# A decode step on one core: w1 in one transfer, w2's first products queued behind V, small constants made on GpSimd

## The chip, the cores and the metric

The kernel runs on one core of one Trainium2 chip. The time is that of the device for one execution, in microseconds (us). A quoted time is the median of several executions on the same chip; the four of each kernel in the first session agree within 0.3% (132.57 to 132.89 us before, 132.71 to 132.92 us changed). A ratio is the mean time of one kernel's runs over the mean time of the other kernel's runs of the same rounds, so it is not quite the ratio of the medians beside it. Executions over 1.5% slower than the fastest of the same kernel are left out of the means.

The core has TensorE (PE; PEld is its weight load), VectorE (DVE), ScalarE (ACT), GpSimd (POOL) and SyncE (SP, which issues most DMA transfers), and 16 DMA engines. A transfer is issued when SyncE gives the order for it. In the trace of the kernel before it gives the orders one after the other, and that for w2's first half (61.08 us) only after a wait of 4.5 us for VectorE's transposes of the block whose space it fills; the order for V's next to it comes at 61.46 us. A transfer then waits in the queue behind those issued earlier: the first packet of w2's first half starts at 64.08 us, while the last packet of K ends at 65.73 us. The engines move it in packets, and each packet has its start, length and size in the trace. The granted clock is the share of TensorE's full clock that the trace shows.

## The reference, cut to what matters

```python
# x: 1x576.  W = 4096 last positions of the cache, 32 query heads, 16 kv heads, Dh = 128
q = x @ wq                                  # wq 576 x 4096
p = softmax(q . k[:, Sk-W:] / sqrt(128))    # 16 x 4096 x 128 of K are read
a = (p . v[:, Sk-W:]) @ wo                  # the same of V; wo 4096 x 576
b = gelu(x @ w1 + b1) @ w2 + b2             # w1 576 x 4608, w2 4608 x 576
g = sigmoid(sum(x * gate_w))
out = g * a + (1 - g) * b
```

One token is computed, so every weight and every cache row is used once. All inputs are bf16; 53.6 MB must come from memory.

## The kernel before

```python
# small rows, issued from ScalarE's queue: x, gate_w, b2, b1
nc.scalar.dma_start(out=x_row, ...)         # ... three more
# large loads, issued from SyncE in this order: w1, wq, K (8 x 2 MB), w2 first half, V (4 x 4 MB), wo, w2 second half
for i0, i1 in ((0, 4), (4, NI)):
    nc.sync.dma_start(out=w1_t[:, i0:i1, :], in_=w1_src[:, i0:i1, :])
nc.sync.dma_start(out=wq_t[:, ...], ...)
# ... constants (identity, parity masks, permutation) on VectorE from one identity matrix ...
# TensorE: h = b1 + x w1 (162 products), q = x wq (144), then scores
for g in range(NG):
    k_t = big.tile([P, 2, SL, Dh], BF16, name="k_t", tag="CDBA"[g])
    # per half: load, two VectorE transposes (2.3 us each), 16 products into s_ps
# ... softmax: maximum on VectorE, two small products, exp on ScalarE, transposes ...
w2_t = big.tile([P, NF, D], BF16, name="w2_t", tag="B")      # the third K block's space
nc.sync.dma_start(out=w2_t[:, 0:NJ, :], in_=w2_src[:, 0])
for g in range(NG):
    v_t = big.tile([P, NCK, Dh], BF16, name="v_t", tag="CDAC"[g])
    # load 4 MB, 128 products into o_ps
# ... wo, and w2's second half in pieces of 10, 6 and 2 rows ...
for f in range(6):
    y_add(gt[:, f : f + 1], w2_t[:, f, :])      # two products of 288 columns each
# ... ov = om . lo32b ...
for f in range(6, NJ):
    y_add(gt[:, f : f + 1], w2_t[:, f, :])
for r in range(RO):
    y_add(ov[:, r : r + 1], wo_t[:, r, :])
for f in range(NJ, NF):
    y_add(gt[:, f : f + 1], w2_t[:, f, :], stop=(f == NF - 1))
```

The scheduler places the 36 products of w2's first half (f below 18) where their data are ready, not where the text has them. In the kernel before that is during the softmax.

## Time and profile before

132.79 us, median of 3 runs (132.57 to 132.89).

| what | value | where it is read |
|---|---|---|
| bytes moved, mean rate | 53.76 MB, 410 GB/s | page |
| K stage, 32 to 64 us | 425 GB/s at a DMA share of 1.00 | table of stretches |
| busy: TensorE, VectorE, ScalarE, GpSimd | 60, 42, 10, 1% of the span | page |
| last weights usable | 128.27 us | chain of waits |

Three rows of the page, the span of 131.2 us in 40 equal slices: granted TensorE clock and DMA share in tenths (9 is 90% or more), and the rate.

```profile
PEclk9999999999999999999999998555555555555589
DMA  7999999899999999999999999989989999999980
GB/s 242 407 454 407 472 466 427 381 425 415 430 425 420 430 440 412 420 440 420 423 462 469 410 390 480 450 380 450 475 380 415 480 385 418 404 422 420 410 330 15
```

The transfers fill the span; nothing else does. The end of the chain of waits (start, length, what) says the same of the finish: a transfer, 16 products, a cast.

```profile
103.54 24.73 DMA w_t<-in_B_w_dram
...
128.31 1.19 PE y_ps L268 x16
129.50 0.43 DVE out_row L515
```

Lines of the timeline (start, length, engine, line, operation, count, idle time before it and what ended that):

```profile
12.85 10.21 PE L294 MATMUL h_ps<-x,w_t 128*128 128x2 bf16 x162
...
26.91 4.00 PE L332 MATMUL q_ps<-x,wq_t 128*128 128x2 bf16 x144 [3.86 <-DMA wq_t<-in_A_wq_dram]
...
61.08 0.33 SPq L443 DMA_DIRECT2D w_t<-in_B_w_dram  x1
...
72.74 1.14 PE L268 MATMUL y_ps<-w_t,gt 128*1 128x288 bf16 x15
...
76.76 0.35 PE L414 MATMUL mb_ps<-ones,mh 1*128 1x1 f32 x2
...
77.34 1.39 ACT L427 ACTIVATE p_t<-s_ps,negm 128x512 bf16<-128x512 f32 x1 [44.78 <-DVE negm L418]
...
117.23 4.00 PE L268 MATMUL y_ps<-wo_t,ov 128*1 128x288 bf16 x32 [1.32 <-DMA wo_t<-in_A_wo_dram]
122.74 3.44 PE L268 MATMUL y_ps<-wo_t,ov 128*1 128x288 bf16 x32 [1.51 <-DMA wo_t<-in_A_wo_dram]
...
128.31 1.15 PE L268 MATMUL y_ps<-w_t,gt 128*1 128x288 bf16 x16 [0.71 <-DMA w_t<-in_B_w_dram]
```

The products of w2's first half start at 72.7 us. Behind V, TensorE waits for wo twice and for w2 once. The wo products go at about 125 ns each (32 in 4.00 us), where the granted clock is 0.5.

### The profile page before, as it was taken

How to read it: one execution, taken by the hardware profiler on the slowest of the kernel's cores; microseconds unless marked ns; L12 is line 12 of the kernel's file. 1: busy time of each engine (PE TensorE's matmuls, PEld its weight loads, DVE VectorE, ACT ScalarE, POOL GpSimd, SP SyncE). 2: the span in 40 equal slices, each digit the busy share in tenths (PEclk: the TensorE clock that was granted, in tenths of full speed). 3: DMA queues.
4: the chain of work that ended last, by engine and by line, in shares of the span. 5: the costliest groups of instructions: out<-in, count | busy, mean ns of one | idle time of the engine just before them, and what ended most of it. 6: DMA issues, size and time to landing. Idle time of an engine off the chain costs nothing.

```text
span 131.2 us, 2379 instructions
## 1 busy us (share of the span) xinstructions
PE 79.0 (60%) x1126; PEld 45.2 (34%) x1062; DVE 55.4 (42%) x80; ACT 13.0 (10%) x25; POOL 0.7 (1%) x6
## 2 busy tenths in 40 slices
PE   0037999075599969769769560006573910949583
PEld 0034999074012212112112140006573910934351
DVE  6059100503988988988986720745000000010001
ACT  3000000003000000000000049950000000000001
POOL 2000000000000000000000000000000000000000
PEclk9999999999999999999999998555555555555589
DMA  7999999899999999999999999989989999999980
GB/s 242 407 454 407 472 466 427 381 425 415 430 425 420 430 440 412 420 440 420 423 462 469 410 390 480 450 380 450 475 380 415 480 385 418 404 422 420 410 330 15
DMA packets 3045, 53.76 MB, mean 410 GB/s; under 512 B 342, under 2 KB 346, under 8 KB 604
## 3 DMA queue, kind: packets, MB, share of 16 engines
q1 hardware_dynamic: 3026, 53.61, 96.4%
q8 instruction: 8, 0.13, 0.4%
q10 hardware_dynamic: 10, 0.01, 0.0%
q14 instruction: 1, 0.01, 0.0%
HBM read 53.62 MB, written 0.00 MB: 409 GB/s over the span
## 4 chain that ended last, share of the span: by engine, by line
DMA 65%; PE 13%; DVE 8%; ACT 8%; issue 4%; SPq 1%; DVEq 0%
DMA k_t<-in_A_k_cache_dram 26%; DMA wq_t<-in_A_wq_dram 20%; DMA w_t<-in_B_w_dram 19%; ACT p_t L427 7%; PE o_ps L476 5%; DVE kt L375 3%; PE q_ps L332 3%; DVE pt L435 2%; DVE m L397 2%; PE s_ps L385 1%; PE y_ps L268 1%; SPq L489 1%; PE t_ps L451 0%; DVE out_row L515 0%; SPq L491 0%
## 5 line engine op out<-in xcount | busy, mean ns | idle before, releaser
L375 DVE STREAM_TRANSPOSE kt<-k_t 128x2048 f32<-128x2048 f32 x16 | 36.0, 2290 | 9.4 <-DMA k_t<-in_A_k_cache_dram 9.4
L385 PE MATMUL s_ps<-kt,qz_flat 128*128 128x512 bf16 x128 | 32.8, 404 | 8.6 <-DVE kt L375 8.6
L476 PE MATMUL o_ps<-pt,v_t 128*128 128x8 bf16 x512 | 14.4, 168 | 10.7 <-issue 7.6
L385 PEld LDWEIGHTS <-qz_flat 128*128 128x128 bf16 x64 | 6.5, 102 | 34.2 <-issue 33.0
L476 PEld LDWEIGHTS <-v_t 128*128 128x128 bf16 x512 | 14.3, 104 | 10.9 <-issue 7.8
L427 ACT ACTIVATE p_t<-s_ps,negm 128x512 bf16<-128x512 f32 x8 | 9.7, 1415 | 44.8 <-DVE negm L418 44.8
L494 DVE TENSOR_TENSOR om<-o_ps,rgh 128x128 bf16<-128x128 f32 x1 | 0.3, 292 | 24.2 <-PE o_ps L476 24.2
L294 PE MATMUL h_ps<-x,w_t 128*128 128x2 bf16 x162 | 10.2, 202 | 0.0
L294 PEld LDWEIGHTS <-w_t 128*128 128x128 bf16 x162 | 10.1, 163 | 0.0
L268 PE MATMUL y_ps<-wo_t,ov 128*1 128x288 bf16 x64 | 7.4, 420 | 2.8 <-DMA wo_t<-in_A_wo_dram 2.8
L451 PE MATMUL t_ps<-ls,ones 128*128 128x32 f32 x2 | 0.6, 396 | 11.9 <-DVE ls L449 11.9
L435 DVE STREAM_TRANSPOSE pt<-p_t 128x2048 bf16<-128x2048 bf16 x2 | 4.6, 2312 | 7.4 <-ACT p_t L427 7.4
L332 PE MATMUL q_ps<-x,wq_t 128*128 128x2 bf16 x144 | 4.0, 166 | 3.9 <-DMA wq_t<-in_A_wq_dram 3.9
L515 DVE CAST out_row<-y_ps 1x288 bf16<-1x288 f32 x1 | 0.4, 446 | 13.4 <-PE y_ps L268 13.4
L268 PEld LDWEIGHTS <-ov 128*1 128x1 bf16 x64 | 3.9, 118 | 6.1 <-issue 2.8
L268 PE MATMUL y_ps<-w_t,gt 128*1 128x288 bf16 x72 | 5.6, 285 | 0.7 <-DMA w_t<-in_B_w_dram 0.7
L332 PEld LDWEIGHTS <-wq_t 128*128 128x128 bf16 x144 | 3.9, 104 | 3.9 <-DMA wq_t<-in_A_wq_dram 3.9
L195 PE MATMUL xs_ps<-one_b,rows 1*128 1x1 bf16 x9 | 0.7, 195 | 7.3 <-DVE rows L192 7.3
L451 PEld LDWEIGHTS t_ps<-ls,ones 128*128 128x128 f32 x2 | 0.5, 310 | 12.2 <-issue 12.2
L514 ACT CAST out_row<-y_ps 1x288 bf16<-1x288 f32 x1 | 0.4, 391 | 42.5 <-PE y_ps L268 42.5
L303 DVE COPY hacc<-h_ps 128x36 f32<-128x36 f32 x1 | 0.2, 195 | 9.4 <-PE h_ps L294 9.4
L268 PEld LDWEIGHTS <-gt 128*1 128x1 bf16 x72 | 3.2, 82 | 2.8 <-issue 1.8
(68 smaller groups left out, 28.7 us busy)
## 6 DMA issues: line engine op xcount, KB each, us to landing
k_t<-in_A_k_cache_dram SPq DMA_DIRECT2D x8, 2048.0 KB, 30.4
v_t<-in_A_v_cache_dram SPq DMA_DIRECT2D x4, 4096.0 KB
wq_t<-in_A_wq_dram SPq DMA_DIRECT2D x1, 4608.0 KB, 25.7
wo_t<-in_A_wo_dram SPq DMA_DIRECT2D x2, 2304.0 KB, 20.1
w_t<-in_B_w_dram SPq DMA_DIRECT2D x1, 2880.0 KB, 14.1
w_t<-in_B_w_dram SPq DMA_DIRECT2D x1, 2592.0 KB, 11.3
w_t<-in_B_w_dram SPq DMA_DIRECT2D x1, 2304.0 KB
w_t<-in_B_w_dram SPq DMA_DIRECT2D x1, 1440.0 KB, 23.1
```

Source lines behind the costliest of these rows:

```text
L195: nc.tensor.matmul(xs_ps[:, i : i + 1], lhsT=xdup[:, i : 2 * D : NI], rhs=one_b[0:1, 0:1], start=(i == 0), stop=(i == NI - 1), skip_group_ ...
L268: nc.tensor.matmul(y_out[s], lhsT=vec, rhs=row[:, s * DH : (s + 1) * DH], start=start, stop=stop, skip_group_check=True,)
L294: nc.tensor.matmul(h_ps[:, j:NF:NJ], lhsT=w1_t[:, i, j:FH:NJ], rhs=x2[:, i, :], start=False, stop=(i == NI - 1 and j == NJ - 1), skip_grou ...
L332: nc.tensor.matmul(q_ps[:, j : Hq : Hq // 2], lhsT=wq_t[:, i, j * Dh : (j + 1) * Dh], rhs=x2[:, i, :], start=(i == 0 and j == 0), stop=(i ...
L375: nc.vector.transpose(out=kt[:, u * half : (u + 1) * half].bitcast(FP32), in_=k_t[:, f, u * SL // 2 : (u + 1) * SL // 2, :] .rearrange("p ...
L385: nc.tensor.matmul(s_ps[:, u * 512 : (u + 1) * 512].rearrange("p (c k) -> p c k", k=32), lhsT=qz[:, h0 // 2, j, :], rhs=kv[:, u * SL // 4 ...
L397: nc.vector.reduce_max(out=m2[:], in_=s_ps[:].rearrange("p (n b) -> p b n", b=2), axis=AX.X)
L427: nc.scalar.activation(out=p_t[:, cs, :, b], in_=s_ps[:].rearrange("p (c k u b) -> p u b c k", k=8, u=2, b=2)[:, f, b % 2], func=ACT.Exp, ...
L435: nc.vector.transpose(out=pt[:, cs, :].rearrange("p c h -> p (c h)"), in_=p_t[:, cs, :, :].rearrange("p c k b -> p (c k b)"),)
L451: nc.tensor.matmul(t_ps[:], lhsT=ones[:], rhs=ls[:], start=True, stop=True)
L476: nc.tensor.matmul(o_ps[:, 8 * g : 8 * g + 8, 0], lhsT=v_t[:, c, :], rhs=pt[:, c, 8 * g : 8 * g + 8], start=(c == 0), stop=(c == NCK - 1),)
L489: nc.sync.dma_start(out=wo_t[:, r0:r1, :], in_=wo_src[:, r0:r1, :])
```

## The change

The intent: fewer and longer packets for w1 (one row of 41,472 B per partition instead of 18,432 and 23,040 B); the constants taken off VectorE; and the 36 products of w2's first half put behind V in TensorE's queue, so that TensorE does not pause before wo arrives. "V uncut" only removes a loop of one pass.

```diff
-    for i0, i1 in ((0, 4), (4, NI)):
-        nc.sync.dma_start(out=w1_t[:, i0:i1, :], in_=w1_src[:, i0:i1, :])
+    nc.sync.dma_start(out=w1_t[:], in_=w1_src)
 ...
-    nc.vector.memset(ones[:], 1.0)                 # and par, alt, lo32, hi4, lo8, pen, perm on VectorE
+    nc.gpsimd.iota(low[:, c0 : c0 + n], pattern=pattern, base=base, channel_multiplier=1)
+    nc.gpsimd.memset(mask[:, c0 : c0 + n], keep)
+    nc.vector.tensor_tensor(out=low[:], in0=low[:], in1=mask[:], op=ALU.bitwise_and)
+    nc.gpsimd.tensor_scalar(out=is0[:], in0=low[:], scalar1=0.0, scalar2=None, op0=ALU.is_equal)
 ... (perm by affine_select, casts and the two small copies merged, gt in one VectorE instruction)
-    nc.vector.memset(qz_flat[:].bitcast(FP32), 0.0)
+    nc.gpsimd.memset(qz_flat[:].bitcast(FP32), 0.0)
 ...
-    for f in range(6):
-        y_add(gt[:, f : f + 1], w2_t[:, f, :])
+    with tc.issue_after(v_last.ins):
+        for f in range(6):
+            y_add(gt[:, f : f + 1], w2_t[:, f, :])
 ...
-    for f in range(6, NJ):
-        y_add(gt[:, f : f + 1], w2_t[:, f, :])
+    with tc.issue_after(ov_mm.ins):
+        for f in range(6, NJ):
+            y_add(gt[:, f : f + 1], w2_t[:, f, :])
```

More of the change, by code (lines that the diff above doesn't have):

```diff
@@ L11 @@
 BF16 = mybir.dt.bfloat16
+I32 = mybir.dt.int32
 ACT = mybir.ActivationFunctionType
@@ L174 @@
     one_b = const.tile([1, 2], BF16, name="one_b")
-    nc.vector.memset(one_b[:], 1.0)
+    nc.gpsimd.memset(one_b[:], 1.0)
+    NCC = 2 * NI + 32 + 4 + 6
+    low = const.tile([P, NCC], I32, name="low")
+    mask = const.tile([P, NCC], I32, name="mask")
+    c0 = 0
+    for base, pattern, keep in (
+        (0, [[1, NI], [1, 2]], 1),
+        (128, [[-1, 32]], 31),
+        (128, [[-32, 4]], 96),
+        (8, [[-2, HB]], 6),
+        (4, [[-2, 2]], 2),
+    ):
+        n = 1
+        for step, num in pattern:
+            n *= num
+        nc.gpsimd.iota(low[:, c0 : c0 + n], pattern=pattern, base=base, channel_multiplier=1)
+        nc.gpsimd.memset(mask[:, c0 : c0 + n], keep)
+        c0 += n
@@ L176 @@
+    nc.vector.tensor_tensor(out=low[:], in0=low[:], in1=mask[:], op=ALU.bitwise_and)
+    is0 = const.tile([P, NCC], FP32, name="is0")
+    nc.gpsimd.tensor_scalar(
+        out=is0[:], in0=low[:], scalar1=0.0, scalar2=None, op0=ALU.is_equal
+    )
+    alt = is0[:, 0 : 2 * NI].rearrange("p (i t) -> p i t", t=2)
+    lo32 = is0[:, 2 * NI : 2 * NI + 32]
+    hi4 = is0[:, 2 * NI + 32 : 2 * NI + 36]
     ones = const.tile([P, P], FP32, name="ones")
-    nc.vector.memset(ones[:], 1.0)
+    nc.gpsimd.memset(ones[:], 1.0)
@@ L178 @@
     ident = const.tile([P, P], BF16, name="ident")
     make_identity(nc, ident[:])
-    ident_f = const.tile([P, P], FP32, name="ident_f")
-    nc.vector.tensor_copy(out=ident_f[:], in_=ident[:])
-    par = const.tile([P, 2], FP32, name="par")
-    nc.vector.reduce_sum(out=par[:], in_=ident_f[:].rearrange("p (a t) -> p t a", t=2), axis=AX.X)
-    alt = const.tile([P, NI + 1], FP32, name="alt")
-    for t in range(2):
-        nc.vector.tensor_copy(
-            out=alt[:, t : NI + 1 : 2], in_=par[:, t : t + 1].to_broadcast([P, (NI + 1) // 2])
-        )
@@ L191 @@
-    for t in range(2):
-        nc.vector.tensor_copy(out=xdup.rearrange("p (d t) -> p d t", t=2)[:, :, t], in_=x_row)
-    xs_ps = ps_m.tile([P, NI], FP32, name="xs_ps", tag="m")
+    perm = const.tile([P, 4, 4, 32], BF16, name="perm")
+    nc.gpsimd.memset(perm[:], 0.0)
+    nc.gpsimd.affine_select(
+        out=perm[:],
+        in_=perm[:],
+        pattern=[[-64, 2], [-1, 2], [0, 4], [-2, 32]],
+        compare_op=ALU.not_equal,
+        fill=1.0,
+        base=0,
+        channel_multiplier=1,
+    )
@@ new lines @@
+    ident_f = const.tile([P, P], FP32, name="ident_f")
+    nc.gpsimd.tensor_copy(out=ident_f[:], in_=ident[:])
+    lo32b = const.tile([P, 32], BF16, name="lo32b")
+    nc.gpsimd.tensor_copy(out=lo32b[:], in_=lo32)
+    pens = const.tile([P, HB + 2], FP32, name="pens")
+    nc.gpsimd.tensor_scalar(
+        out=pens[:],
+        in0=is0[:, 2 * NI + 36 : NCC],
+        scalar1=1e30,
+        scalar2=-1e30,
+        op0=ALU.mult,
+        op1=ALU.add,
+    )
+    pen = pens[:, 0:HB]
+    pen2 = pens[:, HB : HB + 2]
@@ L194 @@
+    nc.vector.tensor_copy(
+        out=xdup.rearrange("p (d t) -> p d t", t=2),
+        in_=x_row.rearrange("p (d o) -> p d o", o=1).to_broadcast([1, D, 2]),
+    )
+    xs_ps = ps_m.tile([P, NI, 1], FP32, name="xs_ps", tag="m")
     for i in range(NI):
         nc.tensor.matmul(
-            xs_ps[:, i : i + 1],
+            xs_ps[:, i, :],
             lhsT=xdup[:, i : 2 * D : NI],
@@ L203 @@
     x2 = const.tile([P, NI, 2], BF16, name="x2")
-    for t in range(2):
-        nc.vector.tensor_tensor(
-            out=x2[:, :, t], in0=xs_ps[:], in1=alt[:, t : t + NI], op=ALU.mult
-        )
-    lo32 = const.tile([P, 32], FP32, name="lo32")
-    nc.vector.reduce_sum(out=lo32[:], in_=ident_f[:].rearrange("p (a t) -> p t a", t=32), axis=AX.X)
-    lo32b = const.tile([P, 32], BF16, name="lo32b")
-    nc.vector.tensor_copy(out=lo32b[:], in_=lo32[:])
-    hi4 = const.tile([P, 4], FP32, name="hi4")
-    nc.vector.reduce_sum(out=hi4[:], in_=ident_f[:].rearrange("p (a t) -> p a t", t=32), axis=AX.X)
-    lo8 = const.tile([P, 8], FP32, name="lo8")
-    nc.vector.reduce_sum(out=lo8[:], in_=ident_f[:].rearrange("p (a c) -> p c a", c=8), axis=AX.X)
-    pen = const.tile([P, HB], FP32, name="pen")
-    nc.vector.reduce_sum(out=pen[:], in_=lo8[:].rearrange("p (b t) -> p b t", t=2), axis=AX.X)
-    nc.vector.tensor_scalar(
-        out=pen[:], in0=pen[:], scalar1=1e30, scalar2=-1e30, op0=ALU.mult, op1=ALU.add
-    )
-    pen2 = const.tile([P, 2], FP32, name="pen2")
-    nc.vector.reduce_max(out=pen2[:], in_=pen[:].rearrange("p (a b) -> p b a", b=2), axis=AX.X)
-    perm = const.tile([P, 4, 4, 32], BF16, name="perm")
-    idv = ident[:].rearrange("p (b l t) -> p b l t", b=2, t=2)
-    for j in range(4):
-        for b in range(4):
-            nc.vector.tensor_copy(out=perm[:, j, b, :], in_=idv[:, j // 2, :, j % 2])
+    nc.vector.tensor_tensor(
+        out=x2[:], in0=xs_ps[:].to_broadcast([P, NI, 2]), in1=alt, op=ALU.mult
+    )
     s0 = const.tile([1, 1], FP32, name="s0")
@@ L258 @@
     nc.vector.tensor_scalar(
-        out=gh[:, 0, :], in0=hi4[:], scalar1=g_t[:, 0:1], scalar2=None, op0=ALU.mult
+        out=gh[:, 0, :], in0=hi4, scalar1=g_t[:, 0:1], scalar2=None, op0=ALU.mult
     )
@@ L322 @@
     nc.vector.reciprocal(out=r_t[:], in_=e_h[:])
-    p1 = const.tile([P, NF], FP32, name="p1")
-    nc.vector.tensor_tensor(out=p1[:], in0=hacc[:], in1=r_t[:], op=ALU.mult)
     gt = const.tile([P, NF], BF16, name="gt")
-    nc.vector.tensor_scalar(out=gt[:], in0=p1[:], scalar1=omg[:, 0:1], scalar2=None, op0=ALU.mult)
+    nc.vector.scalar_tensor_tensor(
+        out=gt[:], in0=hacc[:], scalar=omg[:, 0:1], in1=r_t[:], op0=ALU.mult, op1=ALU.mult
+    )
     q_ps = ps_m.tile([P, Hq], FP32, name="q_ps", tag="m")
@@ L397 @@
     nc.vector.reduce_max(out=m2[:], in_=s_ps[:].rearrange("p (n b) -> p b n", b=2), axis=AX.X)
-    nc.vector.tensor_tensor(out=m2[:], in0=m2[:], in1=pen2[:], op=ALU.add)
+    nc.vector.tensor_tensor(out=m2[:], in0=m2[:], in1=pen2, op=ALU.add)
     m1 = const.tile([P, 1], FP32, name="m1")
@@ L418 @@
     nc.vector.tensor_tensor(
-        out=negm[:], in0=pen[:], in1=mb_ps[:].to_broadcast([P, HB]), op=ALU.add
+        out=negm[:], in0=pen, in1=mb_ps[:].to_broadcast([P, HB]), op=ALU.add
     )
@@ L448 @@
     ls = const.tile([P, Hq], FP32, name="ls")
-    nc.vector.tensor_scalar(out=ls[:], in0=lo32[:], scalar1=sm[:, 0:1], scalar2=None, op0=ALU.mult)
+    nc.vector.tensor_scalar(out=ls[:], in0=lo32, scalar1=sm[:, 0:1], scalar2=None, op0=ALU.mult)
     t_ps = ps_m.tile([P, Hq], FP32, name="t_ps", tag="m")
@@ L468 @@
         )
-        for u in range(1):
-            n = NCK
-            nc.sync.dma_start(
-                out=v_t[:, u * n : (u + 1) * n, :].rearrange("p c d -> p (c d)"),
-                in_=src[:, :, u * n * Dh : (u + 1) * n * Dh],
-            )
+        nc.sync.dma_start(out=v_t[:].rearrange("p c d -> p (c d)"), in_=src)
         for c in range(NCK):
-            nc.tensor.matmul(
+            v_last = nc.tensor.matmul(
                 o_ps[:, 8 * g : 8 * g + 8, 0],
@@ L496 @@
     )
-    for f in range(6):
-        y_add(gt[:, f : f + 1], w2_t[:, f, :])
+    with tc.issue_after(v_last.ins):
+        for f in range(6):
+            y_add(gt[:, f : f + 1], w2_t[:, f, :])
     ov_ps = ps_m.tile([P, RO], FP32, name="ov_ps", tag="m")
-    nc.tensor.matmul(
+    ov_mm = nc.tensor.matmul(
         ov_ps[:], lhsT=om[:].rearrange("p h a -> p (h a)"), rhs=lo32b[:], start=True, stop=True
```

## The prediction

> **What bounds the kernel now.** The DMA queue. The page counts 53.76 MB at a mean of 410 GB/s, a DMA share of 8 or 9 tenths in nearly every slice, and 65% of the chain that ended last is DMA. In the table of stretches the K stage (32 to 64 us) moves 423 to 428 GB/s at a DMA share of 1.00. The last weight transfer lands at 128.27 us; after it only 16 products (1.15 us), a cast (0.45 us) and the store remain. TensorE is busy 60%, VectorE 42%, and they wait for data.
>
> The queue never runs dry: the third K block is issued at 23.1 us, when transfers up to about 43 us are queued; the last V block at 96.3 us, when queued work reaches about 102 us; wo at 102.2 us, when V lands at 111.7 us.
>
> **What the change does.**
> 1. w1 in one transfer: the same bytes, but 128 packets of 41,472 B instead of 256 of 18,432 and 23,040 B. In the packet records 16,384 B take 614 ns and 32,768 B take 1216 ns, so a packet costs about 12 ns plus its bytes at 27.2 GB/s. Eight packets fewer on each engine save about 0.1 us (an estimate from those records), on the critical path.
> 2. The price: w1's first products wait for all of w1, about 15 us instead of 12.85. They run at 63 ns each (162 in 10.2 us), so they end near 25 instead of 23.06 us, before wq lands at 26.9. Nothing is lost.
> 3. Constants to GpSimd: some 20 small VectorE instructions before 13.7 us go. VectorE then idles 9.4 us before the GELU anyway. GpSimd gets longer and may finish near 10 us; x2 needs its mask by 15 us. Off the path.
> 4. The 36 products of w2's first half now run at 72.7 to 77.9 us, inside the softmax's chain. They leave it, so exp starts up to 0.9 us earlier, which DMA hides. They go behind V: 12 after 115.3 us, 24 after the small ov product. At the granted clock of 0.5 there a product takes about 120 ns (32 in 4.0 us), so 36 need up to 4.3 us; the tail's idle times are 1.3 + 1.5 + 0.7 = 3.5 us (waits for wo and w2). [...] the trace agrees for the tail (uninterrupted from 122.7, granted 1.0 from about 125.8 us). Uninterrupted products from 115.3 us should raise it by about 120 us, so the wo products take some 65 ns rather than 115, and the queue is caught up before 126 us. The last 16 still wait for the last DMA.
> 5. V uncut: the same four transfers as before; no effect.
>
> **Predicted.** 132.79 - 0.1 (packets), and 0 to +0.5 from the tail: 132.7 us, range 132.2 to 133.4. Faster by over 2%: 0.02; same: 0.95; slower: 0.03.
>
> **What would show each step.** Last w2 landing at 128.1 to 128.3 us. h_ps products from about 15 to 25 us. Exp starting before 77. After V, 36 products without idle, clock 1.0 from about 120 us instead of 126, wo products near 65 ns, and TensorE again waiting for DMA before the last 16.
>
> **What would make it wrong.** The clock staying at 0.5 in the tail, or an instruction stall among the queued products (V shows 2.3 us stalls after about 128 products): the end slips 1 to 2 us. Small rows landing so late behind 41 KB packets that wq's products are over 10 us late. The engines finishing the last transfers less evenly.

## The result, and the profile after

132.84 us (132.71 to 132.92, 4 runs) against 132.77 us (132.57 to 132.89, 4 runs); ratio 1.0006, 95% interval 0.9989 to 1.0023. That is the same time. A second session gave 1.0004 (0.9975 to 1.0033).

The page's rows of the changed kernel (span 131.0 us), then its chain of waits, cut:

```profile
PEclk9999999999999999999999965555555555556999
DMA  7999899899999999999999999999999989999980
GB/s 215 481 470 456 362 439 450 356 435 425 420 430 425 425 425 430 430 425 425 440 424 492 400 420 470 410 410 460 425 400 455 460 375 400 433 427 419 407 329 26
```

```profile
1.91 13.59 DMA rows<-in_B_b_dram
...
15.54 1.27 PE h_ps L304 x18
16.82 1.05 PE y_ps L290 x4
17.86 10.14 PE h_ps L316 x162
...
101.27 26.86 DMA w_t<-in_B_w_dram
...
128.17 1.20 PE y_ps L290 x16
129.36 0.43 DVE out_row L534
```

The timeline:

```profile
17.80 10.21 PE L316 MATMUL h_ps<-x,w_t 128*128 128x2 bf16 x162
27.86 3.98 PE L354 MATMUL q_ps<-x,wq_t 128*128 128x2 bf16 x144
...
61.24 0.34 SPq L465 DMA_DIRECT2D w_t<-in_B_w_dram  x1
...
76.98 0.55 PE L436 MATMUL mb_ps<-ones,mh 1*128 1x1 f32 x2 [0.71 <-DVE mh L428]
...
77.76 1.39 ACT L449 ACTIVATE p_t<-s_ps,negm 128x512 bf16<-128x512 f32 x1 [44.22 <-DVE negm L440]
...
119.53 2.63 PE L290 MATMUL y_ps<-wo_t,ov 128*1 128x288 bf16 x32
122.61 2.12 PE L290 MATMUL y_ps<-wo_t,ov 128*1 128x288 bf16 x32 [0.45 <-DMA wo_t<-in_A_wo_dram]
126.07 1.39 PE L290 MATMUL y_ps<-w_t,gt 128*1 128x288 bf16 x20 [1.34 <-DMA w_t<-in_B_w_dram]
128.17 1.15 PE L290 MATMUL y_ps<-w_t,gt 128*1 128x288 bf16 x16 [0.70 <-DMA w_t<-in_B_w_dram]
```

The two ends are the same end: the last 16 products still wait 0.7 us for a transfer, which is usable at 128.13 instead of 128.27 us. In the tail TensorE starts wo 2.3 us later, has caught up by 124.7 us, and waits again. At the front the w1 products begin 5 us later, at 17.8 us, and their first release is not w1 but the small row b1. VectorE is busy 51.8 instead of 55.4 us, GpSimd 5.6 instead of 0.7 us, and neither shows in the time.

### The profile page after: what moved, and what is told of

Same layout as the page of the kernel before. It is cut to its first block, busy times and chain, and to the rows that moved or that the text cites. A ratio compares the mean times of both kernels' runs of the same rounds, so it can differ in the third digit from the quotient of the medians.

```text
span 131.0 us, 2371 instructions
## 1 busy us (share of the span) xinstructions
PE 77.3 (59%) x1126; PEld 44.7 (34%) x1062; DVE 51.8 (40%) x48; ACT 13.0 (10%) x25; POOL 5.6 (4%) x25
## 4 chain that ended last, share of the span: by engine, by line
DMA 57%; PE 22%; DVE 8%; ACT 8%; issue 3%; SPq 1%; ACTq 1%; DVEq 0%
DMA k_t<-in_A_k_cache_dram 26%; DMA w_t<-in_B_w_dram 20%; DMA rows<-in_B_b_dram 10%; PE h_ps L316 8%; ACT p_t L449 7%; PE o_ps L493 5%; DVE kt L397 3%; PE q_ps L354 3%; DVE pt L457 2%; DVE m L419 2%; PE y_ps L290 2%; PE s_ps L407 1%; PE h_ps L304 1%; SPq L506 1%; PE t_ps L473 0%
## 5 line engine op out<-in xcount | busy, mean ns | idle before, releaser
L407 PE MATMUL s_ps<-kt,qz_flat 128*128 128x512 bf16 x128 | 32.0, 397 | 8.6 <-DVE kt L397 8.6
L290 PE MATMUL y_ps<-w_t,gt 128*1 128x288 bf16 x72 | 7.2, 362 | 2.0 <-DMA w_t<-in_B_w_dram 2.0
L290 PE MATMUL y_ps<-wo_t,ov 128*1 128x288 bf16 x64 | 4.8, 306 | 0.4 <-DMA wo_t<-in_A_wo_dram 0.4
L290 PEld LDWEIGHTS <-ov 128*1 128x1 bf16 x64 | 3.1, 91 | 2.2 <-issue 0.7
## 6 DMA issues: line engine op xcount, KB each, us to landing
w_t<-in_B_w_dram SPq DMA_DIRECT2D x1, 2592.0 KB, 11.3
```

Source lines behind the costliest of these rows:

```text
L290: nc.tensor.matmul(y_out[s], lhsT=vec, rhs=row[:, s * DH : (s + 1) * DH], start=start, stop=stop, skip_group_check=True,)
L407: nc.tensor.matmul(s_ps[:, u * 512 : (u + 1) * 512].rearrange("p (c k) -> p c k", k=32), lhsT=qz[:, h0 // 2, j, :], rhs=kv[:, u * SL // 4 ...
```

## The experiments

The theory: the DMA queue bounds the kernel, and all that the change moves lies in time that the queue hides. The rival: parts of the change gain and lose by half a microsecond or more and cancel. A second rival for the front: the chain through b1, w1, wq and K, which the changed kernel's chain of waits lists, is itself a limit.

| run | median us (runs) | before, same rounds | ratio (95%) |
|---|---|---|---|
| w1 whole alone | 132.76 (6) | 132.81 | 0.9999 (0.9962 to 1.0035) |
| queued w2 products alone | 132.64 (6) | 132.81 | 0.9974 (0.9946 to 1.0003) |
| GpSimd constants alone | 132.76 (6) | 132.81 | 1.0002 (0.9965 to 1.0040) |
| half of the last V block unread | 128.14 (4) | 132.81 | 0.9631 (0.9598 to 0.9665) |
| front longer by 5.3 us | 134.70 (4) | 132.64 | 1.0164 (1.0144 to 1.0185) |
| front longer by 10.8 us | 138.83 (3 fast; 139.08 with the slow one) | 132.64 | 1.0453 (1.0402 to 1.0504) |
| 72 queued products | 133.13 (4) | 132.64 | 1.0043 (1.0019 to 1.0067) |
| 144 queued products | 135.98 (4) | 132.64 | 1.0253 (1.0209 to 1.0296) |
| the changed kernel again | 132.85 (6) | 132.77 | 1.0004 (0.9975 to 1.0033) |
| V first | 132.89 (6) | 132.77 | 1.0011 (0.9975 to 1.0048) |
| V first, front longer by 5.3 us | 134.43 (4) | 132.77 | 1.0112 (1.0077 to 1.0147) |
| V first, 72 queued products | 132.99 (4) | 132.77 | 1.0004 (0.9975 to 1.0033) |

### Each part alone

w1 in one transfer, everything else as before:

```diff
-    for i0, i1 in ((0, 4), (4, NI)):
-        nc.sync.dma_start(out=w1_t[:, i0:i1, :], in_=w1_src[:, i0:i1, :])
+    nc.sync.dma_start(out=w1_t[:], in_=w1_src)
```

> The kernel before with one part of the change alone: w1 in one transfer. Theory (the DMA queue bounds, nothing else moves the end): ratio to before 0.998 to 1.001; the last w2 transfer lands 0.1 to 0.15 us earlier than in before's profile; the small rows come later than in before (x near 7.4 us, b1 near 15.5 us, two 41 KB packets or about 3 us apart), so the w1 products run from about 17.5 to 28 us, and that costs nothing. Rival (parts that gain and lose cancel in the whole change): this part alone would be faster by 0.5 us or more, ratio 0.996 or less.

The same time. Its timeline has the late rows: VectorE's first instruction on gate_w starts at 9.90 us (7.82 before), that on b2 at 13.10 us (10.03 before):

```profile
9.90 0.75 DVE L231 CUSTOM_DVE_ANT_0 rows<-rows 1x576 bf16<-1x576 bf16 x1 [2.44 <-DMA rows<-in_gate_w_dram]
13.10 0.51 DVE L253 TENSOR_SCALAR b2g<-rows,omg 1x576 f32<-1x576 bf16 x1 [1.03 <-DMA rows<-in_B_b_dram]
```

The rows are 3.1 to 3.3 us apart, two packets of w1 (a packet of 41,472 B takes 1533 ns in the records). The w1 products started at 16.1 us, 1.4 us earlier than expected here.

The queued w2 products alone: the last two hunks of the change's diff, on the kernel before.

> The kernel before with one part alone: the 36 products of w2's first half issued behind V. Theory: ratio 0.999 to 1.002; the clock falls to 0.5 near 76 us instead of 81.5 us, and exp starts 0.1 to 0.3 us later than in before (77.34 us), not earlier; after V the clock is back at 1.0 near 120 us, the wo products are 65 to 82 ns apart instead of about 115, and TensorE waits 0.7 us for DMA before the last 16. Rival (the tail pays for the products and w1 pays it back): 0.5 us or more slower, ratio 1.004 or more.

The same time by the interval, if anything less (0.3% by the means, 0.17 us by the medians); the rival's half microsecond of loss is not there. Exp starts at 77.92 us, and the second small product of the softmax takes 0.55 us and not the 0.35 us of before, at a clock that has already fallen (0.50 from 76 to 80 us in the table of stretches):

```profile
77.13 0.55 PE L414 MATMUL mb_ps<-ones,mh 1*128 1x1 f32 x2 [0.71 <-DVE mh L406]
```

So the early products had not held up the softmax. Two later runs, half of the last V block unread and 72 queued products, show it more cleanly: they too have the products behind V, but in them the clock fell only at 78.05 and 78.07 us, after the small product (here the first of the two):

```profile
76.89 0.35 PE L436 MATMUL mb_ps<-ones,mh 1*128 1x1 f32 x2 [0.71 <-DVE mh L428]
```

From the start of VectorE's maximum to exp they took 4.56 and 4.55 us, before 4.50, the queued products alone 4.90. So the products cost nothing where they were, and where the clock fell before the small product this stretch was 0.2 to 0.5 us longer. Of the eight kept runs with the front as it is and the products behind V it did so in six (4.76 to 4.97 us), of the three with the early products in none. The moment differs from run to run, and that the early products keep the clock up is not shown.

The GpSimd constants alone: the changed kernel with w1 in two transfers and without the two `issue_after` blocks.

> The changed kernel with w1 in two transfers again and the w2 products free to go early again: only the GpSimd constants and the small merges of VectorE work remain. Theory: ratio to before 0.999 to 1.001; VectorE has 3 to 4 us less work, its wait for K grows or its idle before the GELU does; rows land as in before (x 6.4 us, b1 11.6 us), w1 products start within 1 us of 12.85 us. Rival: a gain or a loss of 0.5 us.

The same time; the w1 products start at 11.77 us. No part shows the gain or loss that the rival needs: the medians of the three differ from before's by 0.05, 0.17 and 0.05 us. The intervals of two of them are 0.4% wide either way, which is half a microsecond, so the rival is excluded only just by the timed runs, and gains of 0.1 us are below what they can see.

### Is it the queue?

```diff
-        nc.sync.dma_start(out=v_t[:].rearrange("p c d -> p (c d)"), in_=src)
+        nv = NCK // 2 if g == NG - 1 else NCK
+        nc.sync.dma_start(out=v_t[:, 0:nv, :].rearrange("p c d -> p (c d)"), in_=src[:, :, 0 : nv * Dh])
 ...
-                lhsT=v_t[:, c, :],
+                lhsT=v_t[:, c % nv, :],
```

> The changed kernel with half of the last V block left unread (2.10 MB of 53.6 MB; its first half is used twice, so the result is wrong on purpose); every engine has the same instructions. Theory (DMA bounds): the time falls by 2.10 MB over the 427 GB/s of the K stage, 4.9 us, to about 127.9 us, ratio 0.963. Rival (a chain of products and waits bounds, and transfers only follow it): a fall under 2 us.

Ratio 0.9631: 4.9 us of 132.8 (4.7 by the medians) for 2.10 MB, as the rate of the K stage gives. With the same instructions on every engine, the time followed the bytes. The result is wrong.

### How much room is in the tail?

The queued products doubled and fourfold (wrong results):

```diff
-        for f in range(6):
+        for f in [*range(NJ)] * 1 + [*range(6)]:      # * 3 for the fourfold one
```

> The changed kernel with the 36 queued w2 products doubled to 72 (wrong result on purpose). Theory: after V the products end near 122 us, wo and w2 catch up at 66 ns a product by about 127.7 us, and TensorE still waits for DMA before the last 16: same time within 0.3 us. Rival (each queued product is paid for at the end): 36 x 0.07 to 0.12 us = 2.5 to 4.3 us slower.

> The changed kernel with 144 queued products, 108 more than it has (wrong result on purpose). Theory: 15 of the extra ones fit at the cold clock and the rest at 66 to 72 ns; the idle times of the tail, 2.7 us in the changed kernel's profile, are used up, and the rest shows: about 4 to 5 us slower (an estimate from 108 products, about 7.2 us, less 2.7 us), with no wait for DMA left before the last 16. Rival (each is paid): 7.2 us or more; no effect: the tail is not bound by TensorE even then.

With 72 products TensorE still waits for DMA before the last 16, as the theory said; but that wait ends at 129.10 us instead of 128.17, and the time is 0.4% longer than before's, at the edge of the 0.3 us that were expected over the changed kernel (which was not run on this chip). The profiled run is the slowest of the four (133.73 us; the others 132.97 to 133.17). Its timeline:

```profile
61.73 0.33 SPq L465 DMA_DIRECT2D w_t<-in_B_w_dram  x1
...
116.01 4.57 PE L290 MATMUL y_ps<-w_t,gt 128*1 128x288 bf16 x48
...
129.10 1.15 PE L290 MATMUL y_ps<-w_t,gt 128*1 128x288 bf16 x16 [0.72 <-DMA w_t<-in_B_w_dram]
```

The loss of this run is not in the tail: the queued products start at 116.01 us, 1.0 us later than the changed kernel's (115.03), before any of the extra ones has run. w2's first half was issued 0.5 us later than in the changed kernel, and in the packet records eight of its first packets took 0.3 to 1.5 us longer than others of their size (774 ns at the median in the changed kernel), and the rate from 64 to 65 us was 310 GB/s, beside 435 and 460. I read this as engines that had no K left when it came. The extra products, which run after 116 us, are no evident cause of a late issue at 61.73 us; the other three runs have no trace. That led to the last group of runs.

With 144 products the wait before the last 16 is gone and all 36 w2 products run in one piece:

```profile
125.76 4.09 PE L290 MATMUL y_ps<-wo_t,ov 128*1 128x288 bf16 x64
...
129.68 2.37 PE L290 MATMUL y_ps<-w_t,gt 128*1 128x288 bf16 x36
```

They end at 132.05 us, 2.7 us later than in the changed kernel, where the 16 end at 129.32 (the profiled run is the fastest of its four; the medians differ by 3.3 us from before's). I had expected 4 to 5 us. The 108 extra products put wo off by 5.9 us (125.76 - 115.32 against 119.53 - 115.03, from V's end to wo's start), 55 ns each and not the 67 ns of my estimate, because all but the first of them run with the clock up (the page's row shows 9 from 117.1 us on); and wo itself then takes 4.09 us instead of 2.63 + 2.12. The mechanism holds, its size was off: about 2.5 us of waits (0.45, 1.34 and 0.70) are the room, and what exceeds it is paid.

### How much room is at the front?

The b1 products and the first four (or all nine) ninths of the w1 products run once more ahead of the real pass; the result is right.

```diff
+    for ni in (4, NI):                 # (NI, NI) for the longer one
     for j in range(NJ):                # b1 products, indented, start=(j == 0)
 ...
-    for i in range(NI):
+    for i in range(ni):                # w1 products, indented
```

> The changed kernel with the b1 products and the first 72 w1 products run once more before the real pass (correct result): the w1 stage ends about 5.5 to 6 us later, near 34 us instead of 28. Theory (the third K block need only be issued before the queue runs out near 43 us): same time as the changed kernel within 0.3 us. Rival (the chain of waits through b1, w1, wq and the third and fourth K blocks is the limit, as the chain of the changed kernel's profile lists it): 5 us slower.

> The changed kernel with the b1 and w1 products run twice: the w1 stage ends about 11.5 us later, near 39.5 us. The third K block is then still issued before 43 us, but the K stage ends some 8 us later, V's first products near 99 us, and the last V block is issued near 103 us, when the queue has run out near 101.5 us. Theory: 1.5 to 4 us slower than the changed kernel, with a hole in the DMA share near 102 us and none before. Rival (front is the limit): 11.5 us slower. No effect at all would say the slack is larger than I read.

Both expectations failed. The front has less room than I read: 5.3 us more cost 1.6%, and 10.8 us cost 4.5%. The longer one shows where. Rows of its table of stretches (from:to, length, busy time of PE, PEld, DVE, ACT and POOL with counts, clock, DMA share, GB/s):

```profile
62.00:64.00 2.00, 1.70 (x9) 0.38 (x4) 2.00 (x2) 0.00 (x0) 0.00 (x0) 1.00 0.96 410
64.00:66.00 2.00, 1.88 (x8) 0.38 (x4) 2.00 (x1) 0.00 (x0) 0.00 (x0) 1.00 0.22 90
66.00:68.00 2.00, 1.82 (x8) 0.38 (x4) 2.00 (x2) 0.00 (x0) 0.00 (x0) 1.00 0.00 0
68.00:70.00 2.00, 1.70 (x9) 0.38 (x4) 2.00 (x2) 0.00 (x0) 0.00 (x0) 1.00 0.64 145
```

The queue is empty around 66 us, not near 102 us: SyncE issued w2's first half at 68.35 us, because its space is that of the third K block and VectorE transposed that block late (SyncE waited 11.3 us for these transposes). Behind it in SyncE's queue stands V's first block, whose space, that of the first K block, had been free since 49.71 us, when VectorE's fourth transpose ended. The narrow place is this one issue. The hole is most of the loss: the four rows moved 1.3 MB where the K stage's rate gives 3.4, which is about 5 us (an estimate) of the 6.0 by which the span grew. In the changed kernel the issue happens at 61.24 us, and the first engine turns to w2 at 63.96 us, 2.4 us before the last K block is usable (66.39 us), with next to nothing to spare.

### The narrow place widened

V's first block is issued ahead of w2's first half; nothing else changes.

```diff
+    v_first = load_v(0)                # the same load, moved here
     w2_t = big.tile([P, NF, D], BF16, name="w2_t", tag="B")
 ...
-        v_t = big.tile(...)            # and its load
+        v_t = v_first if g == 0 else load_v(g)
```

> The changed kernel once more, as the measure for the three runs that share its chip: ratio to before 0.998 to 1.002. In the profile the first w2 packet starts near 63.5 us without a late start (no packet there over 0.1 us longer than its size), because w2's first half was issued by 61.3 us.

> The changed kernel with one line moved: V's first block is issued ahead of w2's first half. It waits only for the first K block's transposes (done at 41.4 us), w2's first half for the third K block's (61.2 us), and K runs out on the fastest engines at 63.5 us. Theory: V is issued near 41.5 us, w2 near 61.2 us with 4.2 MB still in front of it; the median is the same as the changed kernel's within 0.3 us, and none of its runs is over 133.2 us. Rival (the order of these two doesn't matter): the same median with as many slow runs. Slower by 0.5 us or more: later w2 is missed somewhere.

> The kernel whose front was 5.3 us longer (1.0164 times before), now with V's first block issued ahead of w2's first half. Theory (its loss came from w2 being issued at 63.3 us, after K had run out): the loss is gone, at most 0.4 us over the changed kernel of this chip; w2 is still issued near 63.3 us. Rival (the chain b1, w1, wq, K is itself the limit, or the extra block of instructions costs): still 1.5 us or more slower.

> The kernel with 72 queued w2 products (1.0043 times before, 132.97 to 133.73 us), now with V's first block issued ahead of w2's first half (wrong result on purpose). Theory (its 0.5 us were lost at 63.5 us, where eight engines had run out of K when w2 arrived, and not in the tail): at most 0.3 us over the changed kernel of this chip. Rival (the 36 extra products are paid for in the tail, or their block of instructions is): still 0.4 to 0.6 us slower.

- The changed kernel again: the time as it was. w2 was issued at 61.45 us, not by 61.3, and one first packet of w2 was 1.1 us late where none was expected, so the place is as narrow as it looked.
- V first: the same median. One of its 6 runs took 133.99 us, so the part of the theory that said no run over 133.2 us falls. Occasional runs of 133.7 to 134.0 us (two in before too, 133.66 and 133.87) come from something else, which stays open.
- V first with 72 queued products: 1.0004, where 1.0043 stood. 36 more products in the tail are free within what the runs resolve: the changed kernel on the same chip has 1.0004 too. That the 0.4% of the old order was this issue is likely and not shown: the profiled run shows it, the two intervals overlap (to 1.0033 and from 1.0019), the chips differ, and without that one run the old ratio is 1.0031.
- V first with the longer front: 1.0112, where 1.0164 stood. The expectation failed: it is 1.6 us over the changed kernel of the same chip by the medians, where the theory allowed 0.4 and the rival (the chain b1, w1, wq, K, or the extra instructions) said 1.5 or more. At most a third of the loss is gone (0.0052 of the 0.0160 that stand above the changed kernel's ratio; 0.4 of 2.1 us by the medians over before; the two runs were on different chips, and their intervals touch). w2 was issued as late as before, but nothing ran dry: none of its packets took over 0.1 us longer than its size, where in the old order twelve took 0.45 to 1.2 us longer:

```profile
44.62 0.53 SPq L469 DMA_DIRECT2D v_t<-in_A_v_cache_dram  x1
63.49 0.34 SPq L475 DMA_DIRECT2D w_t<-in_B_w_dram  x1
...
129.39 1.15 PE L290 MATMUL y_ps<-w_t,gt 128*1 128x288 bf16 x16 [0.71 <-DMA w_t<-in_B_w_dram]
```

What remains in the profile is the wait that ends at 129.39 instead of 128.17 us, though the packets' total time per engine is that of the changed kernel (126.94 and 126.93 us). So some engine ends later than the rest. I sorted the packet records into 16 back-to-back runs, one for each engine (most packets start 3 or 4 ns before the end of the one ahead of them), and counted the packets of 16,384 B that each brought of the queue that the page calls "instruction" (8 packets, 0.13 MB; here "blocks"). In both records such a block took 1.06 us at the median, a data packet of the same size 0.61 us. For the kernels before and after every packet found its place:

```
last data packet's end, us from the first packet's start
                     engines without a block     engines with one
before               7: 125.6 to 125.9           9: 126.7 to 127.6 (one of them an 8 KB load)
changed              8: 125.3 to 126.3           8: 127.0 to 127.4
```

In the changed kernel the eight engines with a block ended 1.4 us after the eight without (means 127.20 and 125.78 us), and the last to end, at 127.4 us, was one of those with a block. The kernel with the 5.3 us longer front has 180 more TensorE instructions (2368 products and weight loads on its page, not 2188) and brings nine blocks before the end (its page: 9 packets, 0.15 MB) where the changed kernel brings eight, in either order of w2 and V. In the run with the longer front and the old order, the last engine to end had brought two blocks (16 of 2560 packets could not be placed). A second sorting gives the same for the run with V first: its last engine ended at 128.63 us, 1.2 us after the changed kernel's last, and had brought two blocks (some packets of two other engines could not be placed). That fits the 1.2 us that remain, but no run changes the number of blocks alone, so it is a reading of the records and not shown; that the chain at the front costs part of it is not excluded.

No version with a right result beat both kernels.

## Why the prediction was right

It was right: 132.84 us against 132.7 predicted, and the chance was on "same". Point by point:

1. **The bound.** Right, and shown: 2.10 MB less took 4.9 us off.
2. **w1's packets, 0.1 us.** Not shown. By the median packet an engine spends 8 times 1533 ns on w1 where it spent 8 times 686 and 8 times 855, which is 0.06 us less; by the means, which count packets that had to wait, it is 13.0 us in both. Nor is an earlier end: the last wait for data ends 0.14 us earlier in the first profile, but the last 16 products start 0.02 us later than before's (128.31 us) in the second profile of the same kernel, and 0.19 us earlier in the run with the queued products alone, which has the old packets. The timed runs cannot see so little.

```profile
128.33 1.14 PE L290 MATMUL y_ps<-w_t,gt 128*1 128x288 bf16 x16 [0.72 <-DMA w_t<-in_B_w_dram]
```

3. **"w1's first products wait for all of w1, about 15 us ... they end near 25".** The result (nothing lost) held, the step failed. They ran from 17.8 to 28.0 us, after wq had arrived. The release was b1's row, used at 15.54 us instead of 11.64 us. In the packet records of the changed kernel the rows start at 5.29, 8.40 and 11.51 us (1,152 B each), 3.1 us apart beside packets of w1 of 1.53 us, and between the last two the same queue moved a packet of 4 B at 9.98 us: two packets of w1 for a row, as I read it, and these had grown. The prediction had this only among the things that might go wrong. The front's room was also read wrongly: I named the third K block, the last V block and wo, and missed w2's first half, which is the narrowest issue of all. The change kept just inside it.
4. **Constants.** Right that they are off the path. GpSimd finished at 15.4 us, not near 10, because its second half waited 9.0 us for one VectorE instruction that sat behind the late rows. One price showed: a VectorE instruction that took 0.51 us before took 2.04 us, from 13.71 to 15.75 us, beside a GpSimd memset of 1.87 us that had begun at 13.57 us, and 2.03 us beside the same memset in the run with half of the last V block unread; where the memset came later (constants alone) it took 0.57 us. No run isolates it.
5. **"They leave it, so exp starts up to 0.9 us earlier".** Wrong: exp started at 77.76 instead of 77.34 us. In the run with the queued products alone it was 77.92 us. The products had cost the softmax nothing (see the queued w2 products alone); in this profile the clock fell at 76.17 us, and the small product takes 0.55 instead of 0.35 us. This is 0.2 of the 0.42 us; 0.16 us are a K block that came later in that profile.
6. **The tail.** Right in each step; only the first 32 wo products, in whose middle the clock rose, took 82 ns each and not 65. Rows of the table of stretches, before and then changed:

```profile
120.00:124.00 4.00, 2.49 (x24) 1.24 (x20) 0.00 (x0) 0.00 (x0) 0.00 (x0) 0.50 0.98 414
124.00:128.00 4.00, 3.57 (x44) 2.02 (x41) 0.00 (x0) 0.00 (x0) 0.00 (x0) 0.82 0.81 330
```

```profile
120.00:124.00 4.00, 3.55 (x54) 2.36 (x52) 0.00 (x0) 0.00 (x0) 0.00 (x0) 0.93 0.95 392
124.00:128.00 4.00, 2.12 (x32) 1.26 (x29) 0.00 (x0) 0.00 (x0) 0.00 (x0) 1.00 0.84 341
```

   The clock (third column from the end) is up about 5 us earlier (at 120.55 us and not 125.46 us), and the second 32 wo products take 66 ns each (2.12 us) instead of 108 (3.44 us). That pays back the late start, and the last 16 wait for DMA in both. In these traces the clock moved after no single length of work or of pause. It rose 2.7 us after steady work began in the tail of before (122.74 to 125.46 us, where the prediction read 125.8) and 5.5 us after the queued products began in the changed kernel (115.03 to 120.55 us). It fell 3.2 us after the last of the early products of before (77.93 to 81.09 us), 3.2 us after the last score product of the changed kernel (72.97 to 76.17 us) and 2.1 us after that of the run with the queued products alone; in the run with the constants alone it fell (77.77 us) while w2's products were still running. In the V stage of the changed kernel 128 pairs of weight load and 8-column product ran without a gap for 3.6 us (from 111.52 us) and the clock stayed at 0.5; with products of 288 columns behind them it rose.

## What to carry to other kernels

When transfers fill the span, cost a change first at the places where the transfer queue is fed: for each issue, compare the moment it becomes possible with the moment the queue in front runs out on its fastest engine, and take the smallest margin. Here one issue had almost none, and work that looked free elsewhere was charged through it; putting a transfer whose space is already free ahead of it took away the late packets in all three traces, and at most a third of the time that the longer front cost. Here longer packets on the large queue (1.53 us each) also went with later small transfers beside it (b1's row used at 15.54 instead of 11.64 us), so check what waits for the small ones.
